# A hand-written order of 1,076 work items: items 300 to 1,075 rearranged, with other groups of two heads in the scores

## The chip, the cores and the metric

The kernel runs on one core of a Trainium2 chip. The metric is the device time of one execution in microseconds (us), as a median over runs. Five engines work beside each other, each through its own queue in program order: PE (TensorE, matrix products), ACT (ScalarE), DVE (VectorE), POOL (GpSimd) and SP (SyncE, which here only issues transfers). An engine that reaches an instruction whose input is not ready waits, and everything behind it in that queue waits too.

## What is computed

Attention of 4 batches, 8 heads, 768 tokens, 64 elements a head, and then a two-layer network on its output:

```
scores = q @ k.T / 8, masked          # heads 0, 2, 6: causal; the other five: causal,
a = softmax(scores)                   #   only the first 4 tokens and the last 64
x = (a @ v), heads side by side       # 3072 x 512
h = x @ w_in                          # 3072 x 2048
g = max(h, 0) + alpha * min(h, 0)
out = g @ w_out                       # 3072 x 512
```

## The kernel before, in words

The work is cut into items with names, and the string `ORDER` (lines 14 to 71) lists all 1,076 of them. Lines 807 to 811 walk through it and let each item emit its instructions. Since every engine takes its instructions in program order, `ORDER` sets the order in each of the five queues at once.

A segment n (0 to 15) is one pair of heads of one batch: n // 4 is the batch, and n % 4 picks the pair out of (2,6), (1,5), (0,4), (3,7). The letters of an item, with the line of its work:

- `Lq`, `Lk`, `Lv` n: SP loads of q, k and v (lines 209 to 246). `Cq`, `Ck`, `Cv` n: casts to bf16 (315, 328, 334, 349), on the engine that the strings CQ, CK and CV name: Cv4 and Cv5 on POOL, later ones on DVE.
- `Tq`, `Tk`, `tq`, `tk` n (to segment 7): transposes on PE (364) and copies out of PSUM on ACT (369 to 395). From segment 8 on SP transposes by DMA instead: `Dq` n (322) and `Dk` n.head (338).
- `S` n.head.part: score matmuls (424 alone, 431 in a group of two heads; 414 up to segment 3). `s`: exponential on ACT (470, 518, 520). `m`: masks by multiplication on DVE (480, 529, 532).
- `A` n.head: weights times v on PE (553). `a`: reciprocal and product on DVE (563, 564). `X` n: the result of a segment, transposed by DMA from SP (572), or by PE (578) for segments 0 to 3 and 15.
- `P` t.f: first layer for token block t (598), four matmuls for each block of 128 features, one for each of the four segments of a batch, in the order n % 4 = 0, 1, 2, 3. `p`: relu on ACT (603). `g`: prelu on DVE (610).
- `O` t.s.quarter: four of the sixteen matmuls of the second layer for 128 tokens (618). `o` t.s: copy out on ACT (624) and the store, issued by POOL for t below 6 (628). `L`, `l`: the last 128 tokens in three cuts (637, 646, 647).

Token blocks 2b and 2b+1 (512 and 256 tokens) belong to batch b. So `P2` and `P3` need X4 to X7, and `P4` and `P5` need X8 to X11.

Scores from segment 4 on are not emitted at once. `one_score` (412) puts them in the list `burst`, and `emit_burst` (418) empties it before the first item that may not stand beside a burst (`beside_burst`, 435). If first and second heads of the pairs have at least 576 score columns each in the list, their matmuls are emitted alternately, each in its own half of the rows of the PE array (line 431), so that the two run at the same time; otherwise they are emitted one after the other (line 424):

```
        if min(columns) < SPLIT:
            for x in burst:
                nc.tensor.matmul(*x[3:6], start=True, stop=True)
...
            while halves[0] or halves[1]:
                hh = min((h for h in range(2) if halves[h]), key=lambda h: at[h])
...
                nc.tensor.matmul(to, keys[own], queries[own], start=True, stop=True)
```

PSUM is one tile `P` of 8 banks. `take` hands out the bank that came free first, `give` returns it; a new order therefore also changes which bank an item gets.

Of the kernel before, what the change touches and what calls it, by code (L numbers as in the profile page):

```python
# [37 lines left out]
P2.14 p2.14 g2.14 Cq8 p3.4 Lq10 Lq11 Dk8.0 P2.10 p2.10 Dk9.1 o1.0 p2.3 g2.3 g3.4 Dk8.1 P3.2 P3.14 P3.12 P2.8 Dq8 P2.1
P3.8 o1.1 p3.2 Dk9.0 Lv10 g2.10 Dq9 p3.14 P2.7 Ck10 g3.2 p3.12 g3.12 g3.14 P2.2 p2.2 g2.2 Cq10 Dq10 P2.11 p2.1 g2.1
p2.11 p2.8 g2.11 P3.6 P2.5 p2.5 g2.5 P2.13 p2.13 g2.8 g2.13 P2.0 p2.0 g2.0 p2.7 P3.0 p3.0 P2.4 S8.0.5 Lv8 Lv11 P2.15  # L40
P2.12 s8.0.5 Cq11 g3.0 p2.15 g2.7 g2.15 S8.0.0 p2.12 g2.12 Ck11 p3.6 S9.0.2 P2.6 p2.6 g3.6 s8.0.0 p2.4 g2.4 g2.6
s9.0.2 p3.8 P3.10 g3.8 p3.10 O3.0.0 O2.0.0 S8.1.5 s8.1.5 O3.0.1 O2.0.1 g3.10 m8.0.0 Cv8 S8.1.3 S9.0.0 S8.0.3 S9.1.1
S8.0.1 S9.1.0 s8.1.3 s9.1.0 s8.0.1 s9.0.0 s8.0.3 m8.0.3 m8.0.1 O2.0.2 O2.0.3 o2.0 Dk10.1 Lv9 m9.0.0 Cv9 m8.0.5 Dk11.0
m9.1.0 m9.0.2 S8.0.4 S9.0.1 S10.1.1 S8.1.4 Dq11 s8.1.4 Lq13 Lk13 O3.0.2 Dk10.0 s9.1.1 s10.1.1 s9.0.1 s8.0.4 O3.0.3
o3.0 Dk11.1 S10.1.0 S10.1.2 m9.0.1 S11.0.2 S9.1.2 S8.0.2 S11.0.0 s9.1.2 Cv10 m9.1.1 A9.0 s11.0.2 s10.1.0 O2.3.0 m9.1.2
A9.1 a9.0 a9.1 X9 s10.1.2 s11.0.0 O2.3.1 Lq15 Lv14 Lq12 S8.1.0 S11.0.1 S10.0.3 m10.1.0 s8.0.2 S10.0.1 S8.1.2 S8.1.1
S10.0.0 O2.3.2 s8.1.2 s8.1.0 m8.1.4 Cq13 s11.0.1 s8.1.1 m11.0.2 m10.1.2 m8.0.4 m11.0.0 A8.0 s10.0.0 m8.1.5 m10.1.1
O2.3.3 a8.0 S11.1.2 S10.0.4 S11.1.0 S10.0.5 S10.0.2 m8.1.3 m11.0.1 s10.0.3 s10.0.1 S11.1.1 s11.1.2 A10.1 s11.1.1
O2.2.0 O2.1.0 s10.0.4 m6.0.2 m10.0.1 Cv11 m8.1.1 m8.1.0 a10.1 m10.0.4 Ck13 m10.0.0 m11.1.2 A11.0 A8.1 O2.1.1 s10.0.2
s10.0.5 o2.3 s11.1.0 Dk13.0 m11.1.1 m10.0.3 m10.0.5 m11.1.0 A10.0 a11.0 a8.1 a10.0 O3.1.0 A11.1 Cq12 O2.2.1 O2.2.2  # L50
# [6 lines left out]
p5.6 s12.0.4 Dk14.0 P5.8 s13.1.0 s12.0.2 p5.8 s12.1.1 m12.0.0 g5.6 O4.3.3 Ck15 p5.10 g5.8 m12.0.1 g5.10 m12.0.4 O5.1.0
Cv13 O5.1.1 O5.1.2 o4.3 Dk14.1 S14.1.1 S14.0.0 S12.1.4 S14.0.1 S14.1.0 S13.0.2 m12.1.1 s14.1.0 s13.0.2 O4.2.0 m12.0.5
A12.0 s14.0.1 s12.1.4 O5.1.3 Dk15.1 s14.1.1 Dk15.0 s14.0.0 a12.0 m14.0.1 Dq15 o5.1 O4.2.1 S13.1.2 S12.1.2 S14.1.2
S14.0.4 m13.1.0 m14.0.0 m13.0.1 S14.0.5 S13.0.0 O4.2.2 O4.2.3 s13.1.2 m13.1.2 m13.1.1 s13.0.0 s14.0.4 s14.0.5 m13.0.2  # L60
S12.1.0 m12.1.5 s14.1.2 S12.1.3 S15.0.0 S14.0.3 m13.0.0 A13.1 o4.2 s12.1.0 s12.1.2 A13.0 s15.0.0 O5.0.0 s12.1.3
s14.0.3 m14.0.4 Cv15 a13.1 O5.0.1 a13.0 S15.0.1 S15.0.2 m12.1.0 S15.1.0 S15.1.2 S15.1.1 S14.0.2 O4.1.0 s15.0.2 s15.1.0
m12.1.4 s14.0.2 s15.1.1 m14.1.1 m14.0.5 m14.1.2 m12.1.3 m14.1.0 A12.1 m14.0.3 A14.1 A14.0 a14.0 s15.1.2 a14.1 m15.0.2
s15.0.1 a12.1 O4.1.1 X13 O4.0.0 O4.0.1 O4.0.2 O4.0.3 m15.0.0 m15.1.1 O4.1.2 m15.0.1 m15.1.2 m15.1.0 A15.0 o4.0 A15.1
a15.0 O4.1.3 a15.1 O5.0.2 X15 O5.0.3 X14 x15 o4.1 o5.0 X12 P6.11 p6.11 P6.2 P6.15 P6.10 p6.10 P7.4 P6.0 P6.1 g6.11
g6.10 p6.1 P6.6 P7.8 p6.15 g6.15 g6.1 p6.0 g6.0 P6.5 p7.4 p6.5 p6.6 g7.4 g6.6 g6.5 P6.3 P6.12 P7.2 p6.3 p6.12 g6.12
# [781 lines left out]
```

## Time and profile before

| what | value |
|---|---|
| median of 3 runs | 228.17 us (227.71 to 228.29) |
| the profiled execution: its time | 228.43 us |
| its span, first to last instruction | 225.8 us |
| PE busy | 221.6 us (98%), 2,005 matmuls |
| DVE busy | 149.1 us (66%) |
| ACT busy | 140.1 us (62%) |
| POOL busy | 45.9 us (20%) |
| DMA queue of SP and ACT (q1) | 89,136 packets, 27.73 MB |

The profile is of one execution. The span is measured from the first to the last instruction; some 2.6 us of the time lie around it. In the trace a matmul's record runs from its start to the modelled end of its pipeline, so records overlap; what a matmul costs the PE is the time from its start to the start of the next.

The list counts from 0; item 300 before is `P1.10`, which PE starts at 48.3 us. All of the span after that is open to the change.

### The profile page before, as it was taken

What the parts mean: (1) busy time and instruction counts of PE and PEld (TensorE: products, weight loads), DVE (VectorE), ACT (ScalarE), POOL (GpSimd) and SP (SyncE); (2) the same over time, 40 slices, a digit from 0 to 9 for tenths busy, and PEclk for the clock granted to TensorE, in tenths of its full rate; (3) what the DMA queues carried; (4) which work ended last, traced back from release to release, by engine and by line L of the source; (5) the groups of instructions that cost most, each with busy time, mean ns of one, the idle gap of its engine ahead of it and who ended that gap; (6) DMA issues with size and microseconds to landing.
All of it is one profiled execution on the core that took longest, in us unless ns stands there. A gap on an engine that the chain in (4) does not pass through costs nothing.

```text
span 225.8 us, 5241 instructions
## 1 busy us (share of the span) xinstructions
PE 221.6 (98%) x2005; PEld 136.5 (60%) x2005; DVE 149.1 (66%) x393; ACT 140.1 (62%) x286; POOL 45.9 (20%) x91
## 2 busy tenths in 40 slices
...
PEclk9999999999999999999999999999999999999999
...
GB/s 201 311 240 214 281 223 285 197 196 231 204 284 182 117 232 231 170 167 190 268 160 177 226 243 129 238 156 117 119 94 38 120 93 0 0 3 1 93 68 119
DMA packets 95417, 37.39 MB, mean 166 GB/s; under 512 B 82440, under 2 KB 93600, under 8 KB 95392
## 3 DMA queue, kind: packets, MB, share of 16 engines
q1 hardware_dynamic: 89136, 27.73, 65.2%
...
## 4 chain that ended last, share of the span: by engine, by line
PE 98%; DVE 0%; issue 0%; DVEq 0%
PE P L598 37%; PE P L618 36%; PE P L553 7%; PE P L431 4%; PE P L414 3%; PE P L688 3%; PE P L364 2%; PE P L637 2%; PE P L424 1%; PE P L502 1%; PE P L578 1%; PE P L463 0%; PE P L362 0%; DVE kT L387 0%; DVE ot L646 0%
## 5 line engine op out<-in xcount | busy, mean ns | idle before, releaser
L610 DVE SCALAR_TENSOR_TENSOR g<-neg,oma,P 128x256 bf16<-128x256 f32 (+1 forms) x128 | 70.9, 608 | 36.9 <-ACT neg L603 36.4
L598 PE MATMUL P<-xT,w_in_b 128*128 128x512 bf16 (+1 forms) x512 | 86.6, 326 | 0.0
L618 PE MATMUL P<-w_out_b,g 128*128 128x512 bf16 x368 | 85.3, 379 | 0.0
L603 ACT ACTIVATE neg<-P 128x512 f32<-128x512 f32 x96 | 54.2, 600 | 26.3 <-PE P L598 20.9
L598 PEld LDWEIGHTS <-w_in_b 128*128 128x128 bf16 x512 | 49.5, 98 | 32.3 <-DVE g L610 0.2
L618 PEld LDWEIGHTS <-g 128*128 128x128 bf16 x368 | 33.9, 98 | 37.2 <-issue 1.0
L470 ACT ACTIVATE eR<-P 128x448 bf16<-128x448 f32 (+4 forms) x63 | 36.9, 635 | 5.8 <-PE P L431 2.5
L624 ACT COPY ot<-P 128x512 f32<-128x512 f32 x23 | 13.9, 605 | 37.1 <-PE P L618 32.3
L628 POOL DMA_DIRECT2D out_dram<-ot x18 | 10.3, 572 | 111.0 <-ACT ot L624 110.8
L518 ACT ACTIVATE eS<-P 128x352 bf16<-128x352 f32 x45 | 20.8, 489 | 3.4 <-PE P L431 3.0
L564 DVE TENSOR_TENSOR xn<-P,rcp 128x448 bf16<-128x448 f32 (+1 forms) x32 | 19.5, 608 | 1.1
L529 DVE TENSOR_TENSOR eS<-eS,ms_near 128x352 bf16<-128x352 bf16 x45 | 14.9, 346 | 0.6 <-ACT eS L518 0.5
L563 DVE RECIPROCAL rcp<-P 128x7 f32<-128x7 f32 (+1 forms) x32 | 6.3, 198 | 10.9 <-PE P L553 10.8
L480 DVE TENSOR_TENSOR eR<-eR,mr_near 128x128 bf16<-128x128 bf16 (+5 forms) x54 | 10.7, 227 | 4.3 <-ACT eR L470 4.1
L414 PE MATMUL P<-qT,kT 128*128 128x192 bf16 (+14 forms) x68 | 11.2, 251 | 0.2 <-DVE kT L387 0.2
L553 PEld LDWEIGHTS <-eS 128*128 128x128 bf16 x260 | 9.5, 97 | 2.3 <-issue 0.6
L553 PE MATMUL P<-vb,eS 128*128 128x65 bf16 x260 | 10.7, 193 | 0.0
L431 PE MATMUL P<-qT,kT 64*128 64x176 bf16 (+10 forms) x168 | 10.5, 252 | 0.0
L431 PEld LDWEIGHTS <-kT 64*128 64x128 bf16 x168 | 6.7, 94 | 6.2 <-issue 5.5
L553 PE MATMUL P<-vb,eR 128*128 128x65 bf16 x276 | 10.5, 193 | 0.0
L553 PEld LDWEIGHTS <-eR 128*128 128x128 bf16 x276 | 9.5, 97 | 1.3
L646 DVE COPY ot<-P 128x128 f32<-128x128 f32 x1 | 0.3, 291 | 14.3 <-PE P L637 14.3
...
## 6 DMA issues: line engine op xcount, KB each, us to landing
...
```

The lines of the kernel that those rows point to most:

```text
L414: nc.tensor.matmul(to, keys, queries, start=True, stop=stop)
L431: nc.tensor.matmul(to, keys[own], queries[own], start=True, stop=True)
L470: nc.scalar.activation(ebuf[n, hh][:, lo:hi].rearrange("p (x c) -> p x c", x=len(parts)), P[:, got[0]:got[0] + len(parts), 0:(hi - lo) // ...
L518: nc.scalar.activation(slots, sc[:, 0:352].rearrange("p (s c) -> p s c", c=176), AF.Exp, scale=scale)
L529: nc.vector.tensor_tensor(slots, slots, ms_near[:, 0:2, :] if m == 0 else ms_near[:, 1:3, :], op=ALU.mult)
L553: nc.tensor.matmul(pav[:, i, :], e[:, o:o + 128], vv[:, j, hh, 0:D + 1], start=(m == 0), stop=(m == len(terms) - 1))
L564: nc.vector.tensor_tensor(xn[n][:, 0:nt, D * hh:D * hh + D], pav[:, :, 0:D], rcp.to_broadcast([128, nt, D]), op=ALU.mult)
L598: nc.tensor.matmul(psg[:, w * i:w * (i + 1)], w_in_b[:, c, 128 * fb:128 * (fb + 1)], xT[:, c, o:o + w], start=(x == 0), stop=(x == 3))
L603: nc.scalar.activation(neg[t, f], bank(held["P", t, f][0]), AF.Relu, scale=-1.0)
L610: nc.vector.scalar_tensor_tensor(g_buf[t % 2][:, fb, 0:w], neg[t, f][:, c], oma[:, fb:fb + 1], bank(got[0])[:, c], op0=ALU.mult, op1=ALU.add)
L618: nc.tensor.matmul(bank(held["O", t, s][0]), g_buf[t % 2][:, f, 128 * s:128 * (s + 1)], w_out_b[:, f, :], start=(f == 0), stop=(f == 15))
L624: nc.scalar.copy(ot, bank(got[0]))
```

## The change

Only the string `ORDER` differs. Its first 300 items are the same, and its last 56. The names between are the same names, each once, in another order. Each engine gets the same instructions in other positions, with the same numbers of matmuls (2,005), weight loads, DVE, ACT and POOL instructions; the queue of SP keeps its order entirely, and the one of POOL changes in one place, where `Cv4` comes behind the store `o0.2`.

In the list of score groups with two heads there are 15 before and 15 after. In batch 1 the last two groups change their members, in batch 2 one group loses `S10.0.1`, which goes to the next, and `S10.0.2` stands alone (before, `S6.0.3` did); in batch 3 only the order inside groups changes.

The core of the diff, with the places that the prediction speaks of:

```diff
-g1.6 ro1 tq6 p1.12 s4.0.2 tk7.0 O0.1.1 O0.2.2 O0.1.2 g1.10 S4.0.4 S4.0.0 S5.1.2 g1.12 S4.0.5 S4.1.4 S4.1.0 s4.0.4
...
-s6.1.0 O0.3.1 a5.1 s4.0.5 O0.3.2 O0.3.3 m4.0.1 m4.0.5 Cv4 tq7 S7.0.0 S6.0.5 S7.1.1 S4.1.1 Lk9 Lk10 Lq9 o0.2 o0.3
-S4.1.3 S7.0.1 A5.0 s4.1.1 s7.0.0 m4.0.0 a5.0 X5 A4.0 s7.0.1 Lk11 s7.1.1 a4.0 s4.1.3 O1.1.0 m4.1.3 Cv7 s6.0.5 m7.0.0
...
-m4.1.4 m7.1.2 m6.1.2 S6.0.3 A4.1 s6.0.0 m6.0.0 m6.0.1 A7.1 O1.1.2 A6.1 s6.0.3 m6.0.4 m6.0.3 s6.0.2 a4.1 a6.1 A6.0 A7.0
-a6.0 O1.1.3 O0.0.0 O0.0.1 O0.0.2 O1.0.2 m10.0.2 O1.0.3 O0.0.3 o0.0 X4 X6 a7.1 a7.0 X7 P2.9 P2.3 p2.9 P3.4 Ck9 Cq9 g2.9
...
-O2.2.3 a11.1 X8 O2.1.2 O3.1.1 O3.1.2 X10 o2.2 O3.1.3 O2.1.3 X11 P4.11 o2.1 P4.14 P5.14 p5.14 P4.4 P4.6 Lk12 P5.0 g5.14
...
-Dk12.0 Dk12.1 Lv12 p4.1 Lk14 Lv13 Lk15 g4.1 P4.7 P4.0 p4.2 g4.2 p4.8 g4.8 p4.0 p4.7 g4.7 P4.15 Cv12 S13.0.1 s13.0.1
-S12.0.5 S12.0.3 P4.3 P5.4 g4.0 s12.0.3 p4.3 s12.0.5 S12.1.5 S12.0.1 S12.0.0 S13.1.1 s13.1.1 Dq14 g4.3 Cq15 Ck14
...
+s4.1.4 s5.1.2 m4.0.1 near0 Lk9 Lk10 Cq7 O0.1.3 o0.1 s4.0.0 O0.3.0 O0.3.1 Cv7 m5.1.2 s4.0.5 Tq7 m4.0.5 S6.1.0 tq7
+s4.0.4 m4.0.4 s6.1.0 O0.2.3 o0.2 A5.1 O0.3.2 O0.3.3 a5.1 Cv4 o0.3 S4.1.1 S7.0.1 S4.1.3 S6.0.5 S7.1.1 S7.0.0 s4.1.3
+s7.1.1 m4.1.4 ro1 m4.0.0 A5.0 a5.0 A4.0 s4.1.1 O1.1.0 s6.0.5 S6.0.4 S7.1.0 S6.1.1 a4.0 m4.1.0 s7.0.0 S7.0.2 S6.0.1
...
+S7.1.2 m6.0.4 m4.1.5 S6.1.2 m4.1.1 s6.1.1 S6.0.0 m4.1.3 Lq8 O1.1.3 near1 s7.0.2 O0.0.0 s7.1.2 Cv6 m7.1.1 m7.1.2 A7.1
+s6.1.2 m6.1.2 m10.0.2 s6.0.3 m7.0.0 s6.0.0 O1.0.0 s4.1.2 A4.1 m7.0.2 A7.0 m6.0.0 m6.1.1 A6.1 m6.0.3 a7.1 Ck9 m6.0.5
+a4.1 a6.1 s6.0.2 X4 A6.0 a6.0 X6 Ck8 a7.0 X7 Lq10 O0.0.1 Cq8 O1.0.1 O0.0.2 O0.0.3 o0.0 O1.0.2 O1.0.3 P2.14 P3.12 P2.9
...
+O2.2.1 Ck13 s11.1.2 m10.0.1 X9 Lq15 m10.0.5 m11.1.1 A10.0 a8.1 O2.2.2 O2.2.3 o2.2 m11.1.2 Lv14 Lq12 Dk13.0 a10.0 A11.1
+a10.1 O2.1.0 O2.1.1 X8 a11.1 X10 X11 Lk12 O2.1.2 O2.1.3 P4.8 p4.8 Cq12 P4.6 p4.6 g4.8 P4.11 P4.14 P4.10 p4.10 P5.2
+p4.14 g4.6 g4.14 Ck12 P4.5 p4.5 g4.5 P4.1 Lq14 Dq12 Dk13.1 p4.1 g4.10 Dq13 P5.12 Lv15 P4.4 Cv14 p5.2 g5.2 p4.4 g4.4
+P5.14 O3.1.3 p5.12 g4.1 Dk12.0 Dk12.1 Lv12 P5.6 g5.12 p4.11 Cq14 p5.14 g4.11 o2.1 p5.6 o3.1 g5.6 g5.14 P4.13 p4.13
+g4.13 P4.0 p4.0 S12.0.3 s12.0.3 S13.0.1 P4.12 p4.12 g4.12 s13.0.1 Lk14 Lv13 P4.2 p4.2 P5.0 g4.0 p5.0 g4.2 g5.0 m12.0.3
...
```

More of the change, by code (lines that the diff above doesn't have):

```diff
@@ L27 @@
 s5.0.0 p0.7 S5.0.2 s5.0.2 Cq4 Tq4 tq4 g0.11 P0.4.2 P0.9 nz0 Ck7.0 S5.1.0 p0.9 g0.9 P1.4 s5.1.0 p1.4 Lv6 S4.0.1 Cq6
-m12.1.2 P0.5.0 s4.0.1 P0.5.1 P0.5.2 P1.12 m5.0.0 g1.4 S4.0.3 g0.7 p0.4 p0.5 m5.1.0 g0.4 g0.5 Cv5 P1.10 S5.0.1 p1.10
-s5.0.1 near0 p0.6 g0.6 O0.1.0 Tq6 s4.0.3 m4.0.3 Tk6 tk6.1 tk6.0 O0.2.0 P1.6 p1.6 m5.0.1 Tk7 tk7.1 Lv4 S4.0.2 O0.2.1
-g1.6 ro1 tq6 p1.12 s4.0.2 tk7.0 O0.1.1 O0.2.2 O0.1.2 g1.10 S4.0.4 S4.0.0 S5.1.2 g1.12 S4.0.5 S4.1.4 S4.1.0 s4.0.4
-s4.0.0 m5.1.1 m4.0.4 s4.1.0 m4.1.0 m5.0.2 O0.1.3 s5.1.2 O0.3.0 O0.2.3 Cq7 m5.1.2 Ck8 Tq7 near1 A5.1 o0.1 S6.1.0 s4.1.4
@@ L37 @@
-a6.0 O1.1.3 O0.0.0 O0.0.1 O0.0.2 O1.0.2 m10.0.2 O1.0.3 O0.0.3 o0.0 X4 X6 a7.1 a7.0 X7 P2.9 P2.3 p2.9 P3.4 Ck9 Cq9 g2.9
[L38 to L50, printed above, removed]
-O2.2.3 a11.1 X8 O2.1.2 O3.1.1 O3.1.2 X10 o2.2 O3.1.3 O2.1.3 X11 P4.11 o2.1 P4.14 P5.14 p5.14 P4.4 P4.6 Lk12 P5.0 g5.14
@@ L52 @@
-Ck12 p4.4 p4.6 p4.11 P4.13 g4.6 p4.14 g4.11 Lq14 g4.14 P5.12 P4.5 P4.12 p4.13 Dq12 o3.1 p5.0 g4.13 Cq14 g5.0 Dk13.1
-p4.5 g4.5 g4.4 Cv14 P4.9 p4.9 g4.9 P4.2 P5.2 Dq13 p5.12 g5.12 P4.10 p5.2 P4.8 P4.1 p4.12 g4.12 g5.2 p4.10 g4.10 Lv15
-Dk12.0 Dk12.1 Lv12 p4.1 Lk14 Lv13 Lk15 g4.1 P4.7 P4.0 p4.2 g4.2 p4.8 g4.8 p4.0 p4.7 g4.7 P4.15 Cv12 S13.0.1 s13.0.1
-S12.0.5 S12.0.3 P4.3 P5.4 g4.0 s12.0.3 p4.3 s12.0.5 S12.1.5 S12.0.1 S12.0.0 S13.1.1 s13.1.1 Dq14 g4.3 Cq15 Ck14
-m12.0.3 O4.3.0 s12.1.5 s12.0.1 O4.3.1 O4.3.2 s12.0.0 p4.15 g4.15 P5.6 P5.10 S12.1.1 S12.0.4 S12.0.2 p5.4 S13.1.0 g5.4
@@ L57 @@
[L57 to L66, printed above, removed]
@@ L67 @@
-p6.2 g6.2 P6.4 p7.8 P7.6 P6.14 g6.3 g7.8 p7.6 p6.4 g7.6 g6.4 P7.10 P6.7 P6.8 p6.8 p6.7 P7.0 P6.9 P6.13 g6.7 p7.2 g7.2
+m12.1.2 P0.5.0 s4.0.1 P0.5.1 P0.5.2 P1.12 m5.0.0 g1.4 S4.0.3 g0.7 p0.4 p0.5 m5.1.0 g0.4 g0.5 Cv5 Tk7 p1.12 m5.0.2 p0.6
+Lv4 Tk6 tk6.1 s4.0.3 P1.10 g0.6 P1.6 p1.6 g1.12 tk7.1 tk7.0 O0.1.0 Tq6 tk6.0 S4.0.2 O0.1.1 O0.1.2 S5.0.1 s5.0.1 tq6
+O0.2.0 O0.2.1 g1.6 O0.2.2 p1.10 S5.1.2 m5.0.1 g1.10 m5.1.1 S4.1.4 m4.0.3 S4.0.4 s4.0.2 S4.0.0 S4.0.5 S4.1.0 s4.1.0
+s4.1.4 s5.1.2 m4.0.1 near0 Lk9 Lk10 Cq7 O0.1.3 o0.1 s4.0.0 O0.3.0 O0.3.1 Cv7 m5.1.2 s4.0.5 Tq7 m4.0.5 S6.1.0 tq7
@@ new lines @@
+s4.0.4 m4.0.4 s6.1.0 O0.2.3 o0.2 A5.1 O0.3.2 O0.3.3 a5.1 Cv4 o0.3 S4.1.1 S7.0.1 S4.1.3 S6.0.5 S7.1.1 S7.0.0 s4.1.3
+s7.1.1 m4.1.4 ro1 m4.0.0 A5.0 a5.0 A4.0 s4.1.1 O1.1.0 s6.0.5 S6.0.4 S7.1.0 S6.1.1 a4.0 m4.1.0 s7.0.0 S7.0.2 S6.0.1
+s7.0.1 m7.0.1 S4.1.5 s7.1.0 m7.1.0 s6.0.4 m6.1.0 Lq9 X5 O1.1.1 O1.1.2 S6.0.3 S6.0.2 s6.0.1 m6.0.1 S4.1.2 Lk11 s4.1.5
+S7.1.2 m6.0.4 m4.1.5 S6.1.2 m4.1.1 s6.1.1 S6.0.0 m4.1.3 Lq8 O1.1.3 near1 s7.0.2 O0.0.0 s7.1.2 Cv6 m7.1.1 m7.1.2 A7.1
+s6.1.2 m6.1.2 m10.0.2 s6.0.3 m7.0.0 s6.0.0 O1.0.0 s4.1.2 A4.1 m7.0.2 A7.0 m6.0.0 m6.1.1 A6.1 m6.0.3 a7.1 Ck9 m6.0.5
@@ new lines @@
+a4.1 a6.1 s6.0.2 X4 A6.0 a6.0 X6 Ck8 a7.0 X7 Lq10 O0.0.1 Cq8 O1.0.1 O0.0.2 O0.0.3 o0.0 O1.0.2 O1.0.3 P2.14 P3.12 P2.9
+p2.9 P2.6 p2.14 Lq11 g2.14 g2.9 p3.12 g3.12 P2.7 P2.10 p2.10 g2.10 P2.1 p2.1 g2.1 Dk8.0 P2.2 Dk9.1 Dk8.1 Cq9 p2.2 g2.2
+p2.7 g2.7 p2.6 P2.3 P2.13 p2.13 g2.6 Ck10 Dq8 Cq10 P2.5 P2.11 Dk9.0 p2.5 P2.4 o1.0 o1.1 g2.5 g2.13 p2.11 g2.11 S8.0.0
+s8.0.0 Lv10 Ck11 P3.4 Dq9 Dq10 Lv8 p2.4 g2.4 Lv11 P2.8 p2.8 P3.2 Cq11 p2.3 p3.2 g3.2 g2.3 P3.0 g2.8 p3.0 g3.0 P2.0
+p2.0 g2.0 S8.1.5 s8.1.5 P3.6 P3.14 p3.14 g3.14 P2.15 p3.6 g3.6 p2.15 g2.15 S9.0.2 s9.0.2 S8.0.5 P2.12 P3.10 P3.8 p3.4
@@ new lines @@
+g3.4 p3.8 Dk10.1 Lv9 O3.0.0 O3.0.1 p2.12 g2.12 O2.0.0 O2.0.1 p3.10 s8.0.5 S9.0.0 g3.8 S8.0.1 S8.0.3 S9.1.1 g3.10
+m6.0.2 S8.1.3 S9.1.0 s9.1.1 m9.1.1 s9.1.0 s8.1.3 O2.0.2 O2.0.3 s8.0.3 S10.1.1 S9.0.1 s9.0.0 S8.1.4 s8.0.1 S8.0.4
+s8.0.4 m9.1.0 m8.1.5 Cv10 s9.0.1 s10.1.1 m9.0.2 m8.0.1 Dk11.0 Cv8 Dq11 O3.0.2 m8.0.0 O3.0.3 S11.0.2 S11.0.0 s8.1.4
+S8.0.2 S10.1.2 S9.1.2 o2.0 Lq13 Lk13 S10.1.0 Cv9 O2.3.0 m9.0.0 s9.1.2 s10.1.0 m9.0.1 m8.0.4 m10.1.1 m9.1.2 Dk10.0
+Dk11.1 o3.0 A9.0 s11.0.0 A9.1 m8.1.4 m8.0.5 O2.3.1 m8.0.3 s8.0.2 A8.0 a9.0 a9.1 s10.1.2 S8.1.1 s11.0.2 S10.0.3 S11.0.1
```

18 lines of the change are left out of this document (16 added, 2 removed).

## The prediction

> **What bounds the kernel now.** I read the page first (busy times, then the chain that ended last), then what each engine waits for, and then the queues of PE, SP and POOL in order of time.
>
> ```profile
> PE 221.6 (98%) x2005; PEld 136.5 (60%) x2005; DVE 149.1 (66%) x393; ACT 140.1 (62%) x286; POOL 45.9 (20%) x91
> PEclk9999999999999999999999999999999999999999
> PE 98%; DVE 0%; issue 0%; DVEq 0%
> ```
>
> PE is busy for 221.6 of 225.8 us, and the chain of work that ended last is PE alone. A busy PE could still be slowed, so I took start-to-start times of its matmuls: 512 columns take 216 ns (eight, 1.73 us, all along the chain), 65 columns 30 ns. From item 300 (48.3 us) on, the starts exceed these paces by about 0.5 us in all, outside the score groups. There is next to nothing to win: all that PE waits for weight loads after 56 us is below.
>
> ```profile
> PEld L618 <- issue: 1.0, 5, 0.3
> PEld L553 <- issue: 0.6, 3, 0.2
> PEld L431 <- DVE g L610: 0.4, 1, 0.4
> PEld L618 <- DVE g L610: 0.3, 1, 0.3
> PEld L598 <- DVE g L610: 0.2, 1, 0.2
> ```
>
> So the change is decided by two things: whether PE's own work gets shorter, and whether the new order makes PE wait. As PE's queue has no slack to make up for it, each wait is added to the time in full.
>
> **Part 1, the score groups.** There are 15 groups of two heads in both orders; a group runs about as long as its longer half. Summed over the groups the longer halves have 18,488 columns before and 18,328 after; 160 columns at 216 ns per 512 are 0.07 us. The score that now stands alone (S10.0.2, 488 columns) replaces another of the same size (S6.0.3). **Sum: -0.1 us.**
>
> **Part 2, waits.** I laid the new queues against a PE that never waits, each step with its duration from the rows of before (ACT and DVE start the next about 0.1 us before a record ends). Nearly all hand-offs keep some cover, like before, where after 55 us 20 results reached PE less than 0.3 us ahead of their use and cost nothing. Four places don't keep it, or just.
>
> *Cv4 behind the store o0.2 (POOL).* POOL takes o0.2's issue first, and that waits for ACT.
>
> ```profile
> 62.76 0.93 POOL L349 CAST vb<-vf 128x896 bf16<-128x896 f32 x1 [1.55 <-DMA vf<-in_v_dram]
> 63.63 0.56 POOL L628 DMA_DIRECT2D out_dram<-ot  x1
> 64.65 0.54 POOL L628 DMA_DIRECT2D out_dram<-ot  x1 [0.45 <-ACT ot L624]
> ```
>
> Before, the cast waited only for its load, and A4.0, its reader, came 6 us later. Now, from the last matmul of Tq7: its end 0.2, ACT still at s4.0.5 0.5, then tq7, s4.0.4, s6.1.0 and o0.2 back to back 2.1, POOL's reaction to ACT 0.3 (64.35 to 64.65), issue 0.5, cast 0.9, hand-off 0.05: 4.6 us. PE reaches A4.0 after S6.1.0 0.2, three quarters of O 2.6, the group 0.8, A5.1 and A5.0 0.8: 4.3 us. **+0.3 us** (bounds 0 and 0.5). Everything on PE stands behind A4.0.
>
> *X7 before P2.14 (SP, DMA).* The fourth matmul of the first P2 item reads X7.
>
> ```profile
> 74.03 6.21 PE L618 MATMUL P<-w_out_b,g 128*128 128x512 bf16 x28
> 72.82 5.90 SPq L572 DMA_TRANSPOSE xT<-xn  x3
> 75.39 0.20 DVE L563 RECIPROCAL rcp<-P 128x7 f32<-128x7 f32 x1
> 75.62 0.62 DVE L564 TENSOR_TENSOR xn<-P,rcp 128x448 bf16<-128x448 f32 x1
> ```
>
> Before, DVE finishes X7's input at 76.24, SP issues it at 77.50 (the issue of X6 kept SP for 2.66 us, the shortest such issue 1.21), it lands at 80.29 by the trace's semaphore updates, and PE reads it at 80.72: 0.43 us to spare. Now A6.0 comes last and 24 matmuls instead of 28 follow. From the last matmul of A7.1, PE needs 3.1 us to the end of A6.0 and 27 x 0.216 = 5.8 to the reader: 8.9. DVE, 0.6 late, does a7.1, Ck9, two masks, a4.1, a6.1, a6.0, Ck8, a7.0 in 5.3 (pairs 0.78, casts 0.54): 5.9; with a landing 2.80 after issue (80.29 - 77.50) and hand-offs of 0.1, 8.8. It just fits. If the issue of X6 again keeps SP 1.4 us longer, X7 is 1.25 late. X4 and X6 start 1.5 to 2 us later than before, when the loads ahead of them (landed at 75.18) are gone, so I take the short issue and a little delay: **+0.2** (0 to 1.25).
>
> *X11 before P4.8.* The same chain: from A11.1's last matmul PE needs 19 x 0.216 = 4.1 us (35 matmuls before); DVE and SP 1.1, landing 2.80 to 3.33 (X11 and X8 in before): 3.95 to 4.5 with the hand-off. The store o2.2 is issued 0.4 us before X11 and shares the DMA engines. **+0.15** (0 to 0.4).
>
> *Dk12.0 before S12.0.3.* The largest.
>
> ```profile
> 122.56 3.92 SPq L572 DMA_TRANSPOSE xT<-xn  x3
> 132.38 2.03 SPq L322 DMA_TRANSPOSE qT<-natq  x1
> 136.92 3.70 SPq L338 DMA_TRANSPOSE kT<-natk  x2
> 146.78 0.70 PE L424 MATMUL P<-qT,kT 128*128 128x176 bf16 x7
> ```
>
> SP keeps its order: X11, Lk12, Lq14, Dq12, Dk13.1, Dq13, Lv15, Dk12.0. From X11's issue (125.24) to the landing of Dk12.0 (142.19) are 16.95 us, without a pause on SP. Now S12.0.3 stands 15 items of PE (each 0.865) after O2.1, and five P items sooner than before. From A11.1's last matmul: PE 3.5 + 13.0 = 16.5. Supply: X11's issue 1.15, then 16.95 as before: 18.1, **1.65 late**. The other end: each issue as short as it occurs (9.6 in all) and the shortest landing of a transpose (2.75) give 13.5, in time by 3. Between: the store queue was in the way before.
>
> ```profile
> 131.41 0.54 POOL L628 DMA_DIRECT2D out_dram<-ot  x1 [3.78 <-ACT ot L624]
> 138.35 0.60 POOL L628 DMA_DIRECT2D out_dram<-ot  x1 [6.40 <-ACT ot L624]
> 130.00:133.00 3.00, 3.00 (x20) 1.73 (x19) 0.00 (x0) 0.58 (x1) 0.54 (x1) 1.00 1.33 240
> 138.00:140.00 2.00, 2.00 (x11) 0.90 (x10) 2.00 (x5) 1.06 (x3) 0.60 (x1) 1.00 1.57 74
> ```
>
> The last two rows are stretches of the span; their last columns are clock, DMA share and GB/s. The DMA engines are full at 130 to 133, and at 138 to 140 they are held while moving 74 GB/s (a 16 KB code load starts at 138.96). The two stores of 256 KB (o2.1 and o3.1 come later now) took about 0.8 us of all DMA engines each; the held stretch remains, as PE's place in its code is the same then. I take half of the lateness off: **+0.75** (0 to 1.65).
>
> **Sum:** -0.1 + 0.3 + 0.2 + 0.15 + 0.75 = +1.3 us. The profiled execution took 228.43 us, 0.26 above the median of 228.17; a difference goes on top of either, so 229.5 for the median.
>
> **The rivals.**
>
> 1. *The transfers keep up.* DMA is the place: with loads and stores out of the way X7, X11 and Dk12.0 land at their shortest, the price is zero, and only Cv4's 0.3 and -0.1 remain: +0.2 to +0.6, 228.5 us, not slower beyond what a measurement of this kernel can tell (0.3%, 0.7 us). It decides at Dk12.0: if its landing is under 15.3 us after X11's issue instead of 16.95. For it: the issue records show backpressure (2.03 and 2.45 where 1.21 is possible). Against: SP had no pause there.
> 2. *The queues run as before.* X6's issue takes 2.66 again and the chain to Dk12.0 16.95: 0.3 + 1.25 + 0.3 + 1.65 - 0.1 = +3.4, 231.6 us. For it: order and sizes of the transfers are the same. Against: less traffic beside them.
> 3. *Faster.* PE recovers the 0.5 us that it now loses and the groups pair better than by columns: at most -0.6, 227.6. Against: all of it would have to come at once, and no wait be added.
> 4. *The clock falls.* The granted clock is full in every slice, but the first matmuls (line 688) start 107 ns apart at 128 columns, later ones 56: the clock can halve, and that stretch lasted 4.1 us (1.2 to 5.3), half of it lost. A wait of over 3 us at one place could bring another: 3.4 + 2.1, 233.7 us. None of my four reaches 1.7. The Trainium skill (TensorE: Matmul & The Clock Gate, Part 1: The HAM clock gate) says that the array falls to half its clock after one idle window of about 3.4 us; by that rule it stays full here.
>
> **How the numbers follow.** Forecast, waits of 0.8 to 2.5 us: 0.50. Rival 1: 0.27. Rival 2, over 2.5: 0.17. Rival 3: 0.03. Rival 4: 0.03. Slower by over 0.3% are the forecast and rivals 2 and 4, 0.70; within 0.3% rival 1, 0.27; faster 0.03. The range takes in rival 1 and most of rival 2: 228.1 to 231.3.
>
> **What would show it.** PE should idle, or its starts be apart, at three or four places: at A4.0 (line 553, near 65 us, released by POOL's cast), in the first P2 item (line 598, near 81, by a transfer), in the first P4 item (near 131) and at S12.0.3 (line 424, near 143), each followed by a lasting shift of all that comes later. POOL's cast near 64 should follow a store. The forecast is wrong if PE shows no such idle time, if it waits for ACT or DVE at places that I took as covered, or if the sum of PE's starts without waits differs by more than 0.2 us.

## The result, and the profile after

The changed kernel takes 230.45 us (median of 6 runs, 229.79 to 230.89); the kernel before took 227.94 us beside it (6 runs, 227.52 to 228.36). The ratio is 1.0108, 95% interval 1.0088 to 1.0129: **slower by 1.1%, 2.5 us**. Now and then an execution of either kernel is disturbed and runs longer; the ratios here leave such runs out, so they can differ from the quotient of two medians.

The profiled execution took 230.41 us, its span is 228.7 us (before: 228.43 and 225.8). First the page of the changed kernel: busy times, granted clock, and the chain that ended last.

```profile
PE 221.1 (97%) x1978; PEld 136.5 (60%) x2005; DVE 149.2 (65%) x393; ACT 140.4 (61%) x286; POOL 45.3 (20%) x91
PEclk9999999999999999999999999999999999999999
PE 53%; DMA 21%; issue 7%; DVE 7%; SPq 6%; POOL 3%; ACT 2%; ACTq 0%; DVEq 0%; POOLq 0%
```

PE works as long as before (27 of its 2,005 matmul records are missing) at full clock, but the chain is no longer PE alone: it now leads through transfers, SP, DVE and POOL. Next PE's own waits of the changed kernel from the view of waits (engine, line, released by: us in all, times, longest).

```profile
PEld L618 <- issue: 1.7, 9, 0.3
PE P L598 <- DVE g L610: 0.8, 2, 0.5
PE P L598 <- DMA xT<-xn: 0.8, 2, 0.5
PEld L553 <- issue: 0.7, 3, 0.3
```

Before, no matmul waited for line 610 or for a transfer of xT in this view. These sums are too small, since a record reaches to the end of the pipeline and hides the first part of a wait. I therefore took start to start: what passes between two matmuls less their pace (216 ns for 512 columns), counted where a releaser ended within 0.1 us ahead. In the queue of PE of the changed kernel the places look like this.

```profile
65.30 0.79 PE L553 MATMUL P<-vb,eR 128*128 128x65 bf16 x21
...
81.89 2.33 PE L598 MATMUL P<-xT,w_in_b 128*128 128x512 bf16 x14 [0.49 <-DMA xT<-xn]
...
98.73 1.91 PE L598 MATMUL P<-xT,w_in_b 128*128 128x256 bf16 x12 [0.49 <-DVE g L610]
100.48 0.72 PE L424 MATMUL P<-qT,kT 128*128 128x176 bf16 x6
101.49 2.77 PE L598 MATMUL P<-xT,w_in_b 128*128 128x512 bf16 x20 [0.29 <-DVE g L610]
...
132.99 1.24 PE L598 MATMUL P<-xT,w_in_b 128*128 128x512 bf16 x5 [0.28 <-DMA xT<-xn]
...
145.33 0.51 PE L424 MATMUL P<-qT,kT 128*128 128x64 bf16 x4
```

| place (start on PE, us) | released by | predicted | measured |
|---|---|---|---|
| A4.0 (65.30) | POOL, Cv4 | 0.3 | 0.28 |
| fourth matmul of P2.14 (81.89) | SP, X7 | 0.2 | 0.66 |
| P3.14 (98.73), S8.0.5 (fourth matmul of the group of 100.48), P2.12 (101.49) | DVE, prelu | none | 0.66 + 0.16 + 0.45 = **1.26** |
| fourth matmul of P4.8 (132.99) | SP, X11 | 0.15 | 0.44 |
| S12.0.3 (145.33) | SP, Dk12.0 | 0.75 | 0 (0.73 to spare) |

With 0.08 us at 52 us these are 2.72 us. To see whether that is all, I measured from one matmul that every kernel here has in the same place (number 541, at 45.8 us, just ahead of item 300) to the end of the last: 177.38 us before, with 0.14 us of waits; 179.94 us after, with 2.72. Without the waits 177.24 and 177.22. **The whole difference between these two executions is waits**, and PE's own work is 0.02 us shorter, where the prediction had 0.07 from the other score groups.

For the first row of the table, the queue of POOL of the changed kernel:

```profile
63.74 0.56 POOL L628 DMA_DIRECT2D out_dram<-ot  x1 [2.27 <-ACT ot L624]
64.30 0.94 POOL L349 CAST vb<-vf 128x896 bf16<-128x896 f32 x1
```

The cast starts where the store's issue ends and is over at 65.24; A4.0 starts at 65.30. For the third row, the one that was not foreseen, the queue of DVE of the changed kernel:

```profile
94.75 0.74 DVE L610 SCALAR_TENSOR_TENSOR g<-neg,oma,P 128x512 bf16<-128x512 f32 x1
97.33 0.56 DVE L315 CAST natq<-qf 128x768 bf16<-128x768 f32 x1 [1.85 <-issue]
97.81 6.63 DVE L610 SCALAR_TENSOR_TENSOR g<-neg,oma,P 128x256 bf16<-128x256 f32 x14
```

DVE stands for 1.85 us in front of one cast (Cq11, line 315), and 14 prelus come behind it without a pause. The view finds no releaser ("issue"). Cq11 writes the buffer of segment 9's q (there are two, used in turn), and Dq9, the transfer that reads that buffer, lands at 97.26 by the trace's semaphore updates, 0.07 us ahead of the cast. So the cast waits until its target is free; its own input, Lq11, had been issued by 83.2. The prelus behind it give PE's banks back, so PE runs out of banks at 98.73. Why Dq9 came late is seen in the queues of SP and POOL of the changed kernel, in this order:

```profile
92.18 3.18 SPq L322 DMA_TRANSPOSE qT<-natq  x2
```

```profile
92.31 1.07 POOL L628 DMA_DIRECT2D out_dram<-ot  x2 [11.83 <-ACT ot L624]
```

Dq9 is issued at 92.18 and takes 5.08 us to land (3.23 before, issued 91.40). Two stores of 256 KB, o1.0 and o1.1, are issued 0.13 and 0.67 us after it; before, they had gone at 86.08 and 87.06. X11, in the fourth row, has one such store ahead of it, o2.2, issued 0.41 us before it:

```profile
129.13 0.54 POOL L628 DMA_DIRECT2D out_dram<-ot  x1 [8.45 <-ACT ot L624]
```

Last the chain to Dk12.0, the queue of SP of the changed kernel, and a stretch 2 us after Dk12.0's issue (last columns: clock, DMA share, GB/s; the share adds up the times of all packets that start in the stretch over 16 engines, so it can pass 1):

```profile
126.16 4.62 SPq L572 DMA_TRANSPOSE xT<-xn  x3
...
136.13 1.29 SPq L322 DMA_TRANSPOSE qT<-natq  x1
...
139.93 2.55 SPq L338 DMA_TRANSPOSE kT<-natk  x2
```

```profile
142.00:144.00 2.00, 2.00 (x15) 1.26 (x13) 2.00 (x5) 1.84 (x4) 0.00 (x0) 1.00 1.32 107
```

X11 is issued at 129.54, Dk12.0 at 139.93, landing 144.60: 15.06 us where before it took 16.95. The records that were long before are short: 1.29 for Dq13's (before 2.03), 2.55 for the two Dk12 (3.70). Of the 1.89 us, 1.29 lie between the two issues (10.39 after 11.68) and 0.60 in Dk12.0's own flight (4.67 after 5.27). The stretch in which the DMA engines are held and move little is still there: a share of 1.32 at 107 GB/s, before 1.57 at 74.

### The profile page after: what moved, and what is told of

Same layout as the page of the kernel before. It is cut to its first block, busy times and chain, and to the rows that moved or that the text cites. A ratio compares the mean times of both kernels' runs of the same rounds, so it can differ in the third digit from the quotient of the medians.

```text
span 228.7 us, 5217 instructions
## 1 busy us (share of the span) xinstructions
PE 221.1 (97%) x1978; PEld 136.5 (60%) x2005; DVE 149.2 (65%) x393; ACT 140.4 (61%) x286; POOL 45.3 (20%) x91
## 4 chain that ended last, share of the span: by engine, by line
PE 53%; DMA 21%; issue 7%; DVE 7%; SPq 6%; POOL 3%; ACT 2%; ACTq 0%; DVEq 0%; POOLq 0%
PE P L618 24%; PE P L598 20%; DMA kf<-in_k_dram 8%; DMA vf<-in_v_dram 5%; PE P L553 4%; DMA qf<-in_q_dram 3%; PE P L431 3%; DMA xT<-xn 3%; DMA qT<-natq 2%; DVE g L610 2%; SPq L242 2%; SPq L223 2%; PE P L637 2%; ACT eR L470 1%; SPq L239 1%
## 5 line engine op out<-in xcount | busy, mean ns | idle before, releaser
L598 PE MATMUL P<-xT,w_in_b 128*128 128x256 bf16 (+1 forms) x501 | 86.4, 325 | 2.1 <-DVE g L610 0.8
L618 PE MATMUL P<-w_out_b,g 128*128 128x512 bf16 x352 | 83.6, 379 | 0.9 <-issue 0.2
L603 ACT ACTIVATE neg<-P 128x512 f32<-128x512 f32 x96 | 55.0, 600 | 31.6 <-PE P L598 23.0
L529 DVE TENSOR_TENSOR eS<-eS,ms_near 128x352 bf16<-128x352 bf16 x45 | 14.4, 336 | 7.9 <-ACT eS L518 7.7
```

Of the source, the lines that this page charges most:

```text
L529: nc.vector.tensor_tensor(slots, slots, ms_near[:, 0:2, :] if m == 0 else ms_near[:, 1:3, :], op=ALU.mult)
L598: nc.tensor.matmul(psg[:, w * i:w * (i + 1)], w_in_b[:, c, 128 * fb:128 * (fb + 1)], xT[:, c, o:o + w], start=(x == 0), stop=(x == 3))
L603: nc.scalar.activation(neg[t, f], bank(held["P", t, f][0]), AF.Relu, scale=-1.0)
L618: nc.tensor.matmul(bank(held["O", t, s][0]), g_buf[t % 2][:, f, 128 * s:128 * (s + 1)], w_out_b[:, f, :], start=(f == 0), stop=(f == 15))
```

## The experiments

**Theory.** The loss is the sum of separate hand-offs: the cast behind the store at A4.0, X7, the prelus behind Cq11 (because two stores lie beside Dq9), and X11 (a store beside it). **Rivals**, for each: DVE is simply too slow around 100 us; loads, not stores, hold the transposes; what is taken away at one place comes back at the next, as the new order has less cover everywhere. Times are medians; each ratio is to the kernel before in the same series, where it took 228.11 us in the first series (four kernels), 227.97 us in the second (four), 227.83 us in the third (one).

### Cq11 later

```diff
-Lv11 P2.8 p2.8 P3.2 Cq11 p2.3 p3.2 g3.2 g2.3 P3.0 g2.8 p3.0 g3.0 P2.0 p2.0 g2.0 S8.1.5
+Lv11 P2.8 p2.8 P3.2 p2.3 p3.2 g3.2 g2.3 P3.0 g2.8 p3.0 g3.0 P2.0 p2.0 g2.0 Cq11 S8.1.5
```

> Cq11 is moved on DVE behind seven prelu instructions; PE, ACT, POOL and SP keep the order of the changed kernel. Theory A (Cq11 stood on DVE until the transfer Dq9 had landed at 97.26 us, and the prelus behind it made PE wait 0.66 + 0.16 + 0.45 = 1.26 us between 98.7 and 101.5 us): DVE's idle 1.85 us before Cq11 and PE's three waits go, and the time falls by 1.1 to 1.3 us, from 230.45 to about 229.2. Rival B (the prelus are late because ACT and DVE have too much work in this stage, and Cq11 only stood where the delay showed): PE waits for the prelu as before, time within 0.3 us. Rival C (the time comes back at the next tight hand-off): the three waits go, another of like size appears before 145 us, time within 0.4 us.

Measured: 229.72 us (12 runs), ratio 1.0061 (1.0029 to 1.0093). The three waits at 98 to 102 are gone; 0.28 at A4.0 and 0.40 at P4.8 stay, X7 had none in this execution. It is the fastest of the twelve (228.05 us), so its waits are not those of the median, which fell by 0.7 us and not by the 1.1 to 1.3 expected. The queue of DVE of this kernel:

```profile
95.16 3.63 DVE L610 SCALAR_TENSOR_TENSOR g<-neg,oma,P 128x256 bf16<-128x256 f32 x7 [0.72 <-ACT neg L603]
98.71 0.55 DVE L315 CAST natq<-qf 128x768 bf16<-128x768 f32 x1
```

DVE now waits for ACT ahead of the prelus, so it has time to spare there and its speed was not the limit. One reservation: in this execution Dq9 landed at 94.46, which would have been early enough for the old place as well. The two kernels with four and with three moves, below, close this: there Dq9 took 5.40 and 6.05 us, and with Cq11 at its later place PE still didn't wait.

### Without the stores o1.0, o1.1 and o2.2

```diff
-        (nc.gpsimd if t < 6 else nc.sync).dma_start(out[r:r + 128, :], ot)
+        (t, s) in ((1, 0), (1, 1), (2, 2)) or (nc.gpsimd if t < 6 else nc.sync).dma_start(out[r:r + 128, :], ot)
```

> The changed kernel without three of its 24 stores: o1.0 and o1.1 (issued by POOL at 92.3 and 92.8 us, beside the transposes Dq9 and Dq10) and o2.2 (issued at 129.1, 0.4 us before X11). These 384 rows of the output stay unwritten, all else is computed. Theory A1 (the stores share the DMA engines with the transposes and delay them): Dq9 lands about 3.2 us after its issue instead of 5.08, Cq11 no longer waits, X11 lands 2.8 us after its issue instead of 3.41; PE's 1.26 us at 98.7 to 101.5 and 0.44 us at 133.0 go, time about 228.8. Rival B1 (Dq9 was late because of the loads queued before it or the code load at 97.17, and X11 by itself): landings as in the changed kernel within 0.3 us, waits stay, time within 0.4 us of 230.45. Mixed: one of the two goes, 230.0 or 229.2.

Measured: 229.16 us, ratio 1.0042 (1.0018 to 1.0066). Both waits that the theory put down to the stores are gone, at 100 us and at P4.8; 0.28 at A4.0 and 0.60 for X7 stay. The queue of DVE of this kernel, with Cq11 at its old place:

```profile
94.68 0.74 DVE L610 SCALAR_TENSOR_TENSOR g<-neg,oma,P 128x512 bf16<-128x512 f32 x1
95.34 0.56 DVE L315 CAST natq<-qf 128x768 bf16<-128x768 f32 x1
```

Dq9 took 3.14 us instead of 5.08 and X11 2.74 instead of 3.41. So the stores make both late. The other traces say how near they have to be: with the nearest store over 4 us ahead (the kernel before and its variant below) Dq9 took 3.23 and 3.57 us; with the first of the two stores issued 0.49 and 0.75 us after Dq9 it stayed at 3.69 and 3.52; with the first from 0.30 ahead to 0.30 after it took 5.08 to 6.05 (five kernels), and with the first 1.18 ahead 4.45. The Trainium skill (DMA: Bandwidth & Descriptors, Issuing engines are not separate DMA queues) says that transfers started by different engines run on the same 16 DMA engines and interleave; this agrees with these flights.

### Cv4 ahead of the store, Ck8 behind a7.0

```diff
-s4.0.4 m4.0.4 s6.1.0 O0.2.3 o0.2 A5.1 O0.3.2 O0.3.3 a5.1 Cv4 o0.3
+s4.0.4 m4.0.4 s6.1.0 O0.2.3 Cv4 o0.2 A5.1 O0.3.2 O0.3.3 a5.1 o0.3
...
-a6.0 X6 Ck8 a7.0 X7
+a6.0 X6 a7.0 X7 Ck8
```

> Two places of the changed kernel: POOL casts Cv4 ahead of the store o0.2, and DVE casts Ck8 behind a7.0. First place: theory A: PE's wait of 0.28 us at 65.3 us goes; rival: Cv4 waits for its load instead and PE waits as long. Second place: if DVE makes X7 late, a7.0 ends 0.54 us sooner, X7 is issued sooner by as much and PE's 0.66 us at 81.9 fall to about 0.1; if SP does (the issues of X4 and X6 keep it until 79.0 us whenever a7.0 is ready), X7 is issued when it was and the 0.66 us stay. Time: 230.45 - 0.28 - 0.54 = 229.6 in the first case, 230.2 in the second.

Measured: 230.89 us, ratio 1.0105 (1.0065 to 1.0144). The wait at A4.0 is gone. The wait for X7 is not: 1.33 us. Measured against PE's work, X7 is issued 0.15 us sooner and not 0.54, right behind X6's issue as in the changed kernel, long after a7.0 is done. So X7 isn't late through the cast Ck8 on DVE ahead of it. The wait grew since PE gets there 0.28 us sooner and X7 flies 3.36 us instead of 2.80. Both expected times (229.6 and 230.2) were missed. In this execution Dq9 took 3.52 us and there was no wait at 100 us.

### The loads of q ahead of X4 moved behind X7

```diff
-m4.1.3 Lq8 O1.1.3
+m4.1.3 O1.1.3
...
-X7 Lq10
+X7 Lq8 Lq10
```

(Cq8, which needs the load, goes to the place ahead of Cq9.)

> The two loads Lq8, which stand on SP right before X4, are issued behind X7, and their cast Cq8 moves from behind a7.0 to before Cq9. Theory S (the issues of X4 and X6 are slow, 1.95 us and a pause, because the loads before them still fill the DMA queue): X4's issue takes 1.2 us, X7 is issued as soon as a7.0 is done (78.0 instead of 79.05), lands near 80.9, and PE's wait of 0.66 us at 81.9 goes: time about 229.8. Rival (the code load of 16 KB at 75.55 us holds SP's issues, whatever is queued): X4's issue is slow again, X7 is issued near 79, the wait stays, time within 0.3 us. Second rival: the later loads make Dq8, Dq9 and the casts behind them late and PE waits longer near 100 us: time above 230.6.

Measured: 231.95 us, ratio 1.0153 (1.0111 to 1.0195). The wait for X7 grew to 1.23 us and those at 100 us to 2.22. The theory that these loads hold X7 fell: X4's issue took 2.13 us without them. The wait for X7 grew because it flew 3.30 us instead of 2.80. The second rival held: Dq8 is issued at 90.21 (87.76 in the changed kernel) and Dq9 at 94.61 (92.18), and Dq9 lands at 99.06 (97.26), in front of Cq11. Why X7 flies longer in this kernel and the one ahead is open. The store o0.0 is issued 0.82 and 0.77 us behind it there, and 0.88 to 0.94 us behind it in four kernels where it flies 2.77 to 2.81, but no run changes that alone.

What the traces of all eleven kernels have in common is something else: a 16 KB code load begins between 74 and 81 us. Where it begins 0.1 to 0.55 us after the issue of one of these transposes, that issue keeps SP 1.71 to 2.66 us (nine kernels; in the kernel before it is X6's, in the changed one X4's, 1.95). Where it begins 0.91 and 1.10 us after X4's issue (two kernels), that issue takes 1.22, and X7 comes in time. X4, X6 and X7 are issued one behind the other, so a late first one makes the last late. The queue of SP, first of the changed kernel (code load at 75.55), then of the one with Cq11 later (75.67):

```profile
75.15 5.12 SPq L572 DMA_TRANSPOSE xT<-xn  x3
```

```profile
74.76 4.29 SPq L572 DMA_TRANSPOSE xT<-xn  x3
```

The three issues take 5.12 us in the one and 4.29 in the other. I couldn't move the code load alone, so this is a coincidence in eleven traces, not a shown cause.

### Three repairs at once

```diff
-O0.2.3 o0.2 A5.1 O0.3.2 O0.3.3 a5.1 Cv4 o0.3
+O0.2.3 Cv4 o0.2 A5.1 O0.3.2 O0.3.3 a5.1 o0.3
...
-P3.2 Cq11 p2.3 p3.2 g3.2 g2.3 P3.0 g2.8 p3.0 g3.0 P2.0 p2.0 g2.0 S8.1.5
+P3.2 p2.3 p3.2 g3.2 g2.3 P3.0 g2.8 p3.0 g3.0 P2.0 p2.0 g2.0 Cq11 S8.1.5
...
-O2.1.2 O2.1.3 P4.8 p4.8
+O2.1.2 O2.1.3 O3.1.3 P4.8 p4.8
...
-P5.14 O3.1.3 p5.12
+P5.14 p5.12
```

> The changed kernel with three single items moved: Cv4 ahead of o0.2, Cq11 behind g2.0, and the quarter O3.1.3 (four matmuls, 0.86 us) ahead of P4.8, between X11's issue and its reader. Theory (the loss is the sum of four separate waits, each a matter of one hand-off): the waits at A4.0 (0.28), at P2's items near 100 us (1.26) and at P4.8 (0.44) are all gone, only X7's (0 to 0.66) stays; 230.45 - 0.28 - 1.26 - 0.44 = 228.5 us, ratio to before 1.000 to 1.003. Rival (a queue that is late for another reason: what is taken away at one place comes back at the next, since PE then gets there earlier): a new wait of 0.3 us or more at another line, 229.2 us or more.

Measured: 229.02 us, ratio 1.0044 (1.0016 to 1.0073). The waits at A4.0, at 100 us and at P4.8 are gone, X7's is 0.67. But three new ones came, all for prelus, 0.14 and 0.22 us at P5 items and 0.42 us at a score of segment 13 (S13.0.1): the wait that the rival named came, with a time between the theory's 228.5 and the rival's 229.2. The profiled execution took 234.08 us, but what it lost against the others lies ahead of matmul 541 (see the end of this section), and the next kernel, profiled at 228.63, has the same three waits. The waits of PE of this kernel:

```profile
PE P L598 <- DMA xT<-xn: 0.5, 1, 0.5
PE P L424 <- DVE g L610: 0.3, 1, 0.3
```

The quarter of 0.86 us that I moved to cover X11 had been giving DVE time further on: waits for prelus behind P4.8 stand in the three kernels that move it and in none that leaves it in its place.

### And a fourth: a quarter between X7 and its reader

```diff
-s6.0.0 O1.0.0 s4.1.2 A4.1 m7.0.2 A7.0
+s6.0.0 s4.1.2 A4.1 m7.0.2 A7.0
...
-X7 Lq10 O0.0.1 Cq8 O1.0.1
+X7 Lq10 O1.0.0 O0.0.1 Cq8 O1.0.1
```

> As the one with three items moved, and the first quarter O1.0.0 (0.86 us of PE) taken from ahead of A4.1, A7.0, A6.1 and A6.0 and put behind them, in front of P2.14. Theory (X7 is late because its chain A4.1 - a4.1 - X4 - X6 - X7 starts late against PE; PE's work in between is what covers it): X4 is issued up to 0.86 us earlier against PE's position, the wait at P2.14's fourth matmul is gone (0.66 before), and no wait over 0.1 us is left after 55 us: 227.8 to 228.2 us, even with the kernel before. Rival (ACT and DVE set when A4.1 can begin, PE would only wait there instead): the wait moves to the A groups or stays at P2.14, 0.3 us or more, 228.3 to 228.9 us.

Measured: 229.08 us, ratio 1.0066 (1.0036 to 1.0095). The wait for X7 is gone, against 0.18 us at an A group (ACT). The three waits for prelus stay, and 0.23 us for Dk12.0 at S12.0.3 came in, because O3.1.3 no longer lies ahead of it and the chain took 15.68 us here. So the cover for X7 did what was expected, and the time came out above both expectations through waits of 0.8 us after P4.8, of which neither spoke.

### The stores put back between X11 and Dk12.0

```diff
-O2.1.2 O2.1.3 P4.8 p4.8 Cq12 P4.6 p4.6
+O2.1.2 O2.1.3 O3.1.3 P4.8 p4.8 Cq12 P4.6 o2.1 p4.6
...
-P4.5 p4.5
+P4.5 o3.1 p4.5
```

(and both out of their old places)

> The changed kernel with the stores o2.1 and o3.1 back in the stretch between X11 and Dk12.0, as they stand in the kernel before (o2.1 behind P4.6, o3.1 behind P4.5, for which O3.1.3 goes ahead of P4.8). Theory (the chain from X11's issue to Dk12.0's landing was 15.06 us instead of 16.95 because these two stores of 256 KB were not beside it): the chain is 16 us or more, Dk12.0 lands at or after PE's reach of S12.0.3, which loses its 0.73 us to spare; a wait there of 0 to 1.2 us. X11's wait goes through the quarter. Time 230.45 - 0.44 + 0 to 1.2 = 230.0 to 231.2 us. Rival (the order of the loads or the place of the code load set it, stores don't matter): the chain stays under 15.4 us, no wait at S12.0.3, 230.0 us.

Measured: 230.37 us, ratio 1.0088 (1.0058 to 1.0117). The chain took 15.14 us: the expectation failed, the rival's number came. From X11's issue to Dk12.0's issue it was longer with the stores (11.33 us, after 10.39), but Dk12.0 itself flew 3.81 us instead of 4.67. The queues of POOL and SP of this kernel, the two stores and the two Dk12:

```profile
135.01 0.54 POOL L628 DMA_DIRECT2D out_dram<-ot  x1 [5.52 <-ACT ot L624]
138.96 0.66 POOL L628 DMA_DIRECT2D out_dram<-ot  x1 [3.41 <-ACT ot L624]
```

```profile
140.69 3.09 SPq L338 DMA_TRANSPOSE kT<-natk  x2
```

S12.0.3 had 0.21 us to spare and didn't wait. X11's wait is gone, and 0.69 us for prelus came at 149 us, as with the three repairs.

### The kernel before without these two stores in the chain

```diff
-X11 P4.11 o2.1 P4.14
+X11 P4.11 P4.14
...
-Dq12 o3.1 p5.0
+Dq12 p5.0
...
-Dk12.0 Dk12.1 Lv12
+Dk12.0 Dk12.1 o2.1 o3.1 Lv12
```

> The kernel before with the stores o2.1 and o3.1 moved out of the stretch between X11 and Dk12.0, behind Dk12.1; nothing else. Theory (the two stores make the chain from X11's issue to Dk12.0's landing longer): it falls from 16.95 us to 15.0 to 15.5, the time stays at 228.1 since PE doesn't wait there. Rival (the code load at 139 us, in the middle of Dk12.0's and Dk12.1's issue, makes it longer, and in the changed kernel it merely came behind): the chain stays at 16 us or more.

Measured: 228.01 us, ratio 0.9996 (0.9977 to 1.0015). The chain fell from 16.95 to 16.04 us: 0.77 of it in the issues, the rest in the flight. That lies between the two expectations. Both runs together: the two stores cost the chain's issues 0.8 to 0.9 us. The other traces bear this out: from X11's issue to Dk12.0's pass 11.68 and 11.33 us in the two kernels that have both stores in this stretch, and 10.3 to 10.9 in the nine that don't; Dq13's issue keeps SP 2.03 and 2.16 us with them and 1.28 to 1.29 without. The flight of Dk12.0 doesn't go with the stores: the two kernels that have them show its shortest and its longest, 3.81 and 5.27 us. It does run with the place of the code load. Where that begins at Dk12.0's issue (the stores put back) the flight is 3.81, where 1.3 us behind it (without three stores) 4.16, and in the nine kernels where it begins 1.8 to 2.7 us behind 4.67 to 5.27. Among these nine the flight doesn't follow the code load any further, and no run moves it alone, so this half stays a coincidence, with its cause open.

### Four repairs without a loss of cover

As the kernel with four moves, but O3.1.3 stays where the change has it, and X11 gets its flight free of the store o2.2 in another way: SP issues that store behind Dk12.1.

```diff
-        (nc.gpsimd if t < 6 else nc.sync).dma_start(out[r:r + 128, :], ot)
+        held.update(late=(out[r:r + 128, :], ot)) if (t, s) == (2, 2) else (nc.gpsimd if t < 6 else nc.sync).dma_start(out[r:r + 128, :], ot)
...
+    item("Z2.2", lambda: nc.sync.dma_start(*held.pop("late")))
...
-Dk12.0 Dk12.1 Lv12
+Dk12.0 Dk12.1 Z2.2 Lv12
```

> The changed kernel with Cv4 ahead of o0.2, Cq11 behind g2.0, the quarter O1.0.0 behind A6.0 (in front of P2.14), and the store of o2.2 issued by SP behind Dk12.1 instead of by POOL 0.4 us ahead of X11; O3.1.3 stays where the change has it. Theory (four separate hand-offs make the whole difference, and the waits that came back with O3.1.3 moved came from its cover being gone at P4 and P5): no PE wait of 0.2 us or more is left after 55 us, 227.8 to 228.3 us, ratio to before 0.999 to 1.002. Rival (the new order has less cover everywhere, any repair brings the next wait): waits of 0.3 us or more in all at lines not yet seen, 228.5 us or more, ratio 1.003 or more.

Measured: 228.83 us (12 runs, 227.07 to 230.97; before 227.83, 227.07 to 231.34), ratio 1.0019 (0.9994 to 1.0044). What is left after 55 us are 0.18 us at an A group and 0.11 us for X7, none of 0.2 us or more, as the theory had it. The ratio lies in the theory's range; the median is above its 228.3, and above the kernel before by more than these waits. The waits of PE of this kernel:

```profile
PEld L618 <- issue: 1.7, 9, 0.3
PE P L364 <- POOL natm L328: 1.7, 1, 1.7
PE P L618 <- issue: 0.2, 1, 0.2
```

No matmul waits for a prelu or a transfer in this view any more. The wait of 1.7 us for POOL at line 364 lies in the first 45 us, which all kernels have in common; it is in three of the eleven profiled executions (1.7 us in that with Cv4 and Ck8 moved too, 3.4 in that of the three repairs). As all orders are the same up to there, I take it for chance and not for a trait of an order. It is also why I compare from matmul 541 on:

| kernel | from matmul 541 to the end | waits in it | difference |
|---|---|---|---|
| before | 177.38 | 0.14 | 177.24 |
| after | 179.94 | 2.72 | 177.22 |
| Cq11 later | 177.98 | 0.77 | 177.21 |
| without three stores | 178.17 | 0.96 | 177.21 |
| Cv4, Ck8 | 179.05 | 1.83 | 177.22 |
| loads later | 181.49 | 4.26 | 177.23 |
| three repairs | 178.66 | 1.54 | 177.12 |
| four repairs | 178.21 | 1.03 | 177.18 |
| stores put back | 180.26 | 3.04 | 177.22 |
| before, without two stores | 177.38 | 0.14 | 177.24 |
| four repairs, late store | 177.59 | 0.36 | 177.23 |

The last column is the same to 0.12 us throughout. So every gain and loss of these executions behind matmul 541 is a sum of named waits, and no order has less work for PE than another. None beats the kernel before, whose waits are 0.14 us.

## Why the prediction was right, and where it was wrong

The sign and the range held (228.1 to 231.3, slower 0.70). The time was 0.95 us above the forecast of 229.5, and its sum was made of the wrong parts. The four named places together cost 1.38 us, where the forecast had 1.4 for them, only because X7 and X11 cost 0.75 more and Dk12.0 0.75 less: that is luck. The rest, 1.26 us, came from a place that the prediction had taken as covered. That is one of its own signs of being wrong ("if it waits for ACT or DVE at places that I took as covered"), so its account of the hand-offs was wrong there, though the range held.

- **What bounds the kernel**, "each wait is added to the time in full": right, as the last table shows. The list there of "all that PE waits for weight loads after 56 us" leaves out the longest line of that view, which belongs to the score groups. It did no harm, since PE's own work came out the same in both orders:

```profile
PEld L431 <- issue: 5.5, 14, 0.4
```

- **The score groups, -0.1:** 0.02. The sign may be right; the size is below what matters.
- **Cv4, +0.3:** right, mechanism and size (0.28), though its terms for PE, as written, add to 4.4 and not 4.3; with the cast ahead of the store it is gone.
- **X7, +0.2:** right place, mis-sized: 0.66. The step that failed is "I take the short issue and a little delay". X4's issue took 1.95 us, not the short 1.22, and that pushed X6 and X7. My reason for the short issue, that the loads ahead would be gone, doesn't decide it: with the last two of them behind X7, X4's issue took 2.13 us. What makes it slow is not shown. Over the five kernels that left this place alone the wait was 0 to 0.67, within the bounds that I gave (0 to 1.25).
- **X11, +0.15:** right place and cause, mis-sized: 0.44. I had named the store beside it and taken 2.80 to 3.33 us for the flight; it was 3.41, and 2.74 without the store.
- **Dk12.0, +0.75, "the largest":** wrong, 0. The chain took 15.06 us, under the 15.3 at which rival 1 decides. The step that failed is "I take half of the lateness off", the size of what the chain would gain. It had counted the chain 1.65 us late and took off some 0.9; 1.89 came off. Of this, 1.29 is in the issues, where taking out the two stores alone is worth 0.8 to 0.9, and 0.60 in Dk12.0's flight, whose cause isn't settled. "The held stretch remains" was borne out (1.32 at 107 GB/s, flight 4.67). Of the 0.73 us to spare, 0.44 comes from PE having waited for X11.
- **"Nearly all hand-offs keep some cover":** the step that cost most, 1.26 us. I had laid the queues out with the flights of before, 3.23 us for Dq9. With 3.23 from 92.18 on, Dq9 would have landed at 95.41, just when DVE reaches Cq11 (its last record ahead ends at 95.49), and nothing would have waited. But the stores o1.0 and o1.1 now lie beside Dq9. I had looked at stores beside X11 and in the Dk12 chain and not here, since no matmul reads Dq9 soon; the reader that mattered was a cast that overwrites its source.
- **The rivals:** rival 1's condition held at Dk12.0, and its time was 2 us short. Rival 2's time (231.6) is 1.15 us off, the forecast's 0.95. The waits, 2.7 us, fall in rival 2's bracket (over 2.5) and not in the forecast's (0.8 to 2.5), but not for its reasons: neither X6's 2.66 nor the 16.95 came back. Rival 4 had no occasion: the clock stayed full (0.999), and the longest wait after 55 us was 0.66 us. What it describes does stand in one trace. In the profiled execution of the three repairs PE waits 3.45 us for POOL, up to 32.49 us, and from 32.47 to 35.88 us the granted clock is half; the waits of 1.67 us at the same place in two other executions leave it full.
